# The decode stream ahead of the MLP: a third raw buffer, an earlier start, a pace by stage, and one slot sooner for the even groups' T4 of w_ch2

## Chip, cores and metric

The kernel runs on one core of a Trainium2 chip. The metric is the time of one execution on the device in microseconds (us). One launch does everything: attention, a gated MLP with a spatial projection, and an MLP.

## What is computed

Four batches of 448 tokens, so 1792 tokens of 768 features; 12 heads of 64 in each batch. The weights w_in, w_out, w_ch1 and w_ch2 reach the kernel as fp64 bits, which it decodes to float32 itself. Every product of the gated MLP and of the MLP is made of three TensorE products, of a high and a low part of each side.

```python
attn = 1 / (1 + exp(-(q @ k.T / sqrt(64) - log(448))));  x = attn @ v        # 4 x 12 heads
h = relu(x @ moe_w_in);  u, v = h[..., :512], h[..., 512:]                  # 768 -> 1024
v_n = (v - mean(v)) / sqrt(var(v) + 1e-6)
v_s = einsum('ts,bsd->btd', w_spatial, v_n) + b_spatial[None, :, None]       # over the 448 tokens
x = (u * v_s) @ w_out                                                        # 512 -> 768
xn = (x - mean(x)) / sqrt(var(x) + 1e-6) * g_ln
out = x + relu(xn @ w_ch1) @ w_ch2                                           # 768 -> 3072 -> 768
```

## The kernel before

The stages follow each other on TensorE (PE): attention to about 222 us, then `hv` and `hu` (x times the two halves of w_in, batch by batch), then `spatial` for four batches, then `Project` (the product with w_out, LayerNorm, transposes), then the MLP.

**Spatial.** Each batch has four tiles of 128 features. A tile is 11 matmuls into one of four PSUM banks: three times `mm3` (L359 to L361, high by high, high by low, low by high) and two more, L706 and L707, for the last 64 tokens. L707 reads `t2`, which the last ACT instruction of `vn_make` (L687) writes. DVE multiplies the bank by u (L709) and so frees it for the tile four later.

**Projection.** PE makes 14 blocks of 128 tokens. For each, ACT copies the bank out (`evac`, L745), DVE subtracts the mean and multiplies by g_ln (L755), ACT scales (L758), and PE transposes (L765) the block of two steps before. g_ln is fetched by SP at L1180.

**MLP.** w_ch1 and w_ch2 are cut in 12 groups of 256 hidden features; each group's two products are done by Strassen's seven products of blocks, whose weight operands bear the names 11, 21, 22, T1, T2, T3, T4. A group has 14 slots. A table gives for each operand the slot at which it is made: `=T4` subtracts two blocks on POOL (L829), `T4` splits it in a high part (cast on ACT, L834) and a low part (subtraction on POOL, or with a `v` on DVE, L837). `W1_JOBS` is for w_ch1 (even groups, odd groups), `W2_JOBS` for w_ch2; the slots of `W2_JOBS` count from 14 behind those of `W1_JOBS`, so an even group's w_ch2 operands are made in the same slots as the next, odd group's w_ch1 operands. DVE also sums finished products (L1417) and adds the hidden features (`summed`, L1321; `s_first` L1352 and L1356; `s_add`, L1340; lows at L1308 and L1312), on which PE's next products wait.

**The decode stream.** A weight chunk (128 x 768 as fp64 bits, 768 KB) is loaded by SP at L371, brought to float32 by ACT in two instructions (L405, L410) and by DVE in one (L414). For the first and the even groups' w_ch2, 12 chunks in all, this is done ahead of the MLP by the generator `after_stream`: it decodes a chunk, stores it to a scratch tensor `wfscr` (384 KB, L1086), and the MLP reads it back with `load_plain` (L822). It has two raw buffers in `q_all`, and a chunk's load is issued on SP as the one before the last is done. It advances by one step per `AFTER_US` of PE's modelled time, from `hv` of the last batch on and only while the queue of w_out's decode jobs is empty; SP issues its DMAs in program order, as ACT and DVE do their instructions.

Of the kernel before, what the change touches and what calls it, by code (L numbers as in the profile page):

```python
# [88 lines left out]
PLACE_W_R = [30464, 28672]  # L89
PLACE_F = dict(y=0, gb=6144, tmp=6912, xn=9216, dec=10752)  # L90
# [34 lines left out]
        (-7, "11"), (-6, "=T1"), (-6, "21"), (-5, "T1"), (-5, "=T3"), (-4, "22"), (-3, "=T2"), (-2, "T2"), (0, "T3"),  # L125
        (0, "=T4"), (2, "T4"),
# [4 lines left out]
        (-5, "11v"), (-4, "=T1"), (-4, "22v"), (-4, "=T3"), (-3, "21v"), (-3, "=T2"), (-2, "=T4"), (-1, "T4v"), (1, "T3"),  # L131
# [13 lines left out]
BY_GPSIMD = (0, 2, 4)  # L145
AFTER_US = 1.15
# [150 lines left out]
def sigmoid_attention_gmlp_mlp(ctx: ExitStack, tc, q, k, v, w_in, w_sp, w_out, g_ln, w1, w2, out):  # L297
# [762 lines left out]
    jobs.add([t.split for t in wo_chunks[:2]])  # L1060
    jobs.add([t.decode for t in wo_chunks[2:]] + [t.split for t in wo_chunks[2:]])
    out2_r.free()
    vraw, uraw, vns, g = {}, {}, {}, []
    put_after[0] = 1
    defer[0] = True

    def after_stream():
        parts = [(g, f) for g in PLAIN_W2 for f in range(2)]

        def load(k):  # L1070
            if k < len(parts):
                g, f = parts[k]
                weights[g].load(1, f, raw_r.next())

        load(0)
        load(1)
        for _ in range(4):
            yield
        for k, (g, f) in enumerate(parts):
# [4 lines left out]
            blk = dec_r.next()  # L1084
            weights[g].bits(1, f, blk)
            nc.sync.dma_start(wfscr[g, f], blk.ap(WC))  # L1086
            load(k + 2)
            yield

    after, owed = after_stream(), [0.0]  # L1090

    def go_on(us):
        owed[0] += us
        while owed[0] >= AFTER_US:
            owed[0] -= AFTER_US
            next(after, None)

# [23 lines left out]
    def filled(gen, every, side=(), pace=1.0):  # L1121
        side = iter(side)
        for i, us in enumerate(gen):
            if not jobs.q:
                go_on(pace * (us or 0.0))
# [20 lines left out]
    filled(hv(B - 1), 3, v_norm(0))  # L1146
# [4 lines left out]
    wsp_raw.free()  # L1151
    vraw_r.blocks.append(F.alloc(4 * DH))
# [3 lines left out]
    filled(hu(B - 1), HU_EVERY, vn_first())  # L1156
# [3 lines left out]
    vu["u"].free()  # L1160
    gf_r = Ring(F, S, 2)
    for b in range(B):
        g_alloc((b + 1) * S)
        side = [*([v_norm(2)] if b == 0 else ()), *([vn_at(b + 2)] if b + 2 < B else ())]
        filled(spatial(b, vns[b], wsp, uraw[b], gf_r, g), 2 if b else 1, chain(*side), (0.75, 0.75, 1.1, 1.1)[b])
# [6 lines left out]
    u_in.free()  # L1172
    jobs.drain()
# [39 lines left out]
    for j, (u, c) in enumerate(order):  # L1213
# [10 lines left out]
        if j > 11:  # L1224
            proj.turn_parked(order[j - 2][1], banks, nc.vector.tensor_copy if j < 13 else nc.scalar.copy)
        proj.evac(c, ps, y_at[c])
# [309 lines left out]
    def at(i, slot):  # L1536
        return 14 * i + slot
# [229 lines left out]
```

## Times and profile before

| what | value |
|---|---|
| runs | 1020.75, 1021.31, 3429.54 us; median 1021.31 |
| the profiled execution | 1022.51 us |
| its span | 1020.7 us |
| PE busy | 990.6 us, 97% |
| DVE, ACT, POOL busy | 748.9 (73%), 497.1 (49%), 371.1 (36%) us |
| mean granted clock of PE | 0.994 |
| read from HBM | 168.54 MB |

The span is the stretch from the first to the last instruction of the profiled execution; its own time is 1.8 us more. PE is busy nearly always, so a gain must come from the stretches in which it stands still or runs at the lower clock: the windows of the stages and the list of PE's waits say where these are, and the timelines of the other engines say what it waits for.

### The profile page before, as it was taken

The page shows a single profiled execution, that of the slowest core. Times are in us where ns is not written, and L with a number is a line of the kernel's source. Part 1 is how long each engine was busy: PE and PEld are TensorE (multiplying, and loading weights), DVE is VectorE, ACT ScalarE, POOL GpSimd, SP SyncE. Part 2 cuts the span into 40 slices and gives each one's busy share as a digit, 9 for nine tenths or more (in the row PEclk, how much of TensorE's full clock was granted, in tenths as well). Part 3 has the DMA queues.
Part 4 walks back from the last instruction along what each step waited for, and adds up shares of the span by engine and source line. Part 5 has one row for each costly group of instructions (what it writes and reads, how often), then busy time and mean ns, then how long its engine had stood idle before and what let it go on. Part 6 is the DMA issues. An engine that isn't in the chain of part 4 may idle for free.

```text
span 1020.7 us, 14832 instructions
## 1 busy us (share of the span) xinstructions
PE 990.6 (97%) x5140; PEld 826.0 (81%) x5140; DVE 748.9 (73%) x985; ACT 497.1 (49%) x826; POOL 371.1 (36%) x331
## 2 busy tenths in 40 slices
PE   8999999999888999999999999999999999999997
PEld 5456667678777998887878788778889999999996
DVE  4669898727585787678888889898876676666666
ACT  5756554435565675456656565644422222222221
POOL 3533233101210585456768767675720021000000
PEclk9999999999998999999999999999999999999999
DMA  8875889746866259966859778695979988888884
GB/s 220 241 237 182 301 298 284 272 152 215 300 230 229 93 191 351 373 241 217 317 205 338 272 262 303 209 340 176 342 289 313 318 272 251 248 248 249 252 249 148
DMA packets 98555, 261.04 MB, mean 256 GB/s; under 512 B 13104, under 2 KB 27440, under 8 KB 98352
## 3 DMA queue, kind: packets, MB, share of 16 engines
q1 hardware_dynamic: 93072, 246.67, 71.4%
q0 software_dynamic: 1760, 7.36, 2.2%
q10 hardware_dynamic: 3648, 6.06, 1.7%
q8 instruction: 41, 0.67, 0.3%
q14 instruction: 34, 0.28, 0.1%
HBM read 168.54 MB, written 91.50 MB: 255 GB/s over the span
## 4 chain that ended last, share of the span: by engine, by line
PE 77%; DVE 6%; issue 4%; DMA 4%; POOL 4%; ACT 4%; SPq 0%; ACTq 0%; POOLq 0%; DVEq 0%
PE ps L359 13%; PE ps L361 13%; PE ps L360 13%; PE acc L359 8%; PE acc L360 8%; PE acc L361 8%; PE psa L569 6%; PE ps L529 5%; POOL f_all L829 2%; POOL t_all L837 2%; PE ps L542 1%; DVE f_all L1417 1%; DMA q_all<-in_w 1%; PE psa L556 1%; DVE f_all L414 1%
## 5 line engine op out<-in xcount | busy, mean ns | idle before, releaser
L1417 DVE TENSOR_TENSOR f_all<-acc,f_all 128x1536 f32<-128x1536 f32 (+1 forms) x106 | 164.6, 1553 | 63.0 <-PE acc L361 62.5
L359 PE MATMUL ps<-r_all,t_all 128*128 128x384 f32 (+1 forms) x432 | 156.9, 363 | 4.1 <-DVE f_all L1321 4.1
L361 PE MATMUL ps<-r_all,t_all 128*128 128x384 f32 (+1 forms) x432 | 156.5, 362 | 0.0
L360 PE MATMUL ps<-r_all,t_all 128*128 128x384 f32 (+1 forms) x432 | 156.3, 362 | 0.0
L1299 ACT CAST r_all<-f_all 128x512 fp32r<-128x512 f32 (+1 forms) x144 | 81.5, 568 | 125.9 <-DVE f_all L1340 83.9
L1312 DVE TENSOR_TENSOR r_all<-f_all,r_all 128x512 fp32r<-128x512 f32 (+1 forms) x143 | 110.4, 780 | 38.1 <-ACT r_all L1299 35.4
L837 POOL TENSOR_TENSOR t_all<-f_all,t_all 128x384 fp32r<-128x384 f32 x78 | 90.3, 1161 | 74.4 <-ACT t_all L834 74.2
L359 PE MATMUL ps<-r_all 128*128 128x512 f32 (+2 forms) x249 | 96.8, 389 | 2.7 <-DVE f_all L709 1.8
L361 PE MATMUL ps<-r_all 128*128 128x512 f32 (+2 forms) x249 | 95.0, 382 | 0.0
L829 POOL TENSOR_TENSOR f_all<-f_all 128x384 f32<-128x384 f32 x76 | 88.9, 1173 | 16.8 <-ACT t_all L834 8.8
L360 PE MATMUL ps<-r_all 128*128 128x512 f32 (+2 forms) x249 | 94.9, 381 | 0.0
L359 PEld LDWEIGHTS ps<-r_all,t_all 128*128 128x128 f32 x432 | 81.2, 188 | 13.8 <-DVE f_all L1321 5.7
L360 PEld LDWEIGHTS ps<-r_all,t_all 128*128 128x128 f32 x432 | 81.3, 188 | 8.1
L361 PEld LDWEIGHTS ps<-r_all,t_all 128*128 128x128 f32 x432 | 81.2, 188 | 8.1
L516 ACT ACTIVATE f_all<-ps,bias_s 128x896 f32<-128x896 f32 x70 | 68.3, 1009 | 35.5 <-PE ps L529 15.0
L360 PE MATMUL acc<-r_all,t_all 128*128 128x512 f32 x198 | 78.4, 396 | 0.1
L361 PE MATMUL acc<-r_all,t_all 128*128 128x512 f32 x198 | 78.3, 395 | 0.0
L359 PE MATMUL acc<-r_all,t_all 128*128 128x512 f32 x198 | 78.2, 395 | 0.0
L834 ACT CAST t_all<-f_all 128x384 fp32r<-128x384 f32 x102 | 50.4, 513 | 34.9 <-POOL f_all L829 29.9
L512 POOL TENSOR_TENSOR r_all<-f_all,r_all 128x384 fp32r<-128x384 f32 x22 | 23.6, 1072 | 115.1 <-DVE r_all L508 111.9
L529 PEld LDWEIGHTS ps<-r_all 64*128 64x128 f32 x432 | 37.5, 184 | 29.9 <-issue 16.9
L359 PEld LDWEIGHTS ps<-r_all 128*128 128x128 f32 x249 | 47.2, 189 | 15.4 <-issue 3.8
(209 smaller groups left out, 2218.4 us busy)
## 6 DMA issues: line engine op xcount, KB each, us to landing
t_all<-wscr SPq DMA_DIRECT2D x164, 384.0 KB, 3.8
wscr<-t_all SPq DMA_DIRECT2D x102, 384.0 KB, 4.1
q_all<-in_w SPq DMA_DIRECT2D x42, 768.0 KB, 6.5
wscr<-r_all SPq DMA_DIRECT2D x66, 384.0 KB, 4.6
r_all<-wscr SPq DMA_DIRECT2D x46, 384.0 KB, 3.9
m_all<-in_v SPq DMA_DIRECT2D x24, 256.0 KB, 3.6
yscr<-f_all SPq DMA_DIRECT2D x14, 384.0 KB, 2.6
f_all<-in_k SPq DMA_DIRECT2D x45, 112.0 KB, 3.6
```

The source lines that it names most:

```text
L359: nc.tensor.matmul(ps, lh, rh, start=first, stop=False, skip_group_check=skip)
L360: nc.tensor.matmul(ps, lh, rl, start=False, stop=False, skip_group_check=skip)
L361: nc.tensor.matmul(ps, ll, rh, start=False, stop=last, skip_group_check=skip)
L516: nc.scalar.activation(af, ps[:, :, :S], AF.Sigmoid, bias=bias_s, scale=1.0 / math.sqrt(D))
L529: nc.tensor.matmul(ps[:, j, :S], a[w][rows, kc], a[x][rows], start=(i == 0), stop=(i == 2))
L569: nc.tensor.matmul(a["ps"][rows, :S], a["v"][:, 4 * j + c], af[:, j], start=(p % 2 == 0 and c == 0), stop=(p % 2 == 1 and c == 2),)
L829: eng.tensor_sub(self.f(m, WHERE[m][name]), self.f(m, a), self.f(m, b))
L834: high(t[:, 0], x)
L837: low.tensor_sub(t[:, 1], x, t[:, 0])
L1299: nc.scalar.copy(t[:, 0], self.rt(name))
L1312: (eng or nc.vector).tensor_sub(t[:, 1], self.rt(name), t[:, 0])
L1417: nc.vector.tensor_add(t, x, t)
```

## The change

It has two parts.

The stream: the first chunk's load goes to a third raw buffer (`extra_raw`, in `f_all`) and is issued as attention ends; the next two loads follow the decode of w_out's last two chunks, whose raw buffers they take. A table `THEN` says which load follows which chunk; chunks 7 and 10 use a further place, `late_raw`, once hu's buffers are free. The stream's pace is a factor by stage, `PACE`; a new chunk is begun only while no other job is queued, but a chunk once begun goes on. `go_until(1)` and `go_until(11)` make sure of a count of chunks at two places; `v_load(1)` stands behind the first.

The MLP: in `W2_JOBS` for even groups all jobs of slots -5 to -1 are one slot sooner; in `W1_JOBS` for odd groups six jobs are one or two slots later, and `load_plain` is one slot sooner. No instruction is added or removed on any engine.

```diff
+THEN = {1: 3, 2: 4, 3: 5, 4: 6, 5: 8, 6: 9, 7: 10, 8: 11}
 W1_JOBS = [ ... ,   # the second list is for odd groups
-        (-7, "11"), (-6, "=T1"), (-6, "21"), (-5, "T1"), (-5, "=T3"), (-4, "22"), (-3, "=T2"), (-2, "T2"), (0, "T3"),
-        (0, "=T4"), (2, "T4"),
+        (-7, "11"), (-6, "=T1"), (-6, "21"), (-4, "T1"), (-3, "=T3"), (-3, "22"), (-2, "=T2"), (-1, "T2"), (0, "T3"),
+        (1, "=T4"), (2, "T4"),
 W2_JOBS = [         # the first list is for even groups
-        (-5, "11v"), (-4, "=T1"), (-4, "22v"), (-4, "=T3"), (-3, "21v"), (-3, "=T2"), (-2, "=T4"), (-1, "T4v"), (1, "T3"),
+        (-6, "11v"), (-5, "=T1"), (-5, "22v"), (-5, "=T3"), (-4, "21v"), (-4, "=T2"), (-3, "=T4"), (-2, "T4v"), (1, "T3"),
+PACE = (1.0, 0.8, 0.5, 0.4, 0.4, 1.0)
...
-    jobs.add([t.split for t in wo_chunks[:2]])
-    jobs.add([t.decode for t in wo_chunks[2:]] + [t.split for t in wo_chunks[2:]])
     out2_r.free()
+    extra_raw = F.at(5760, 2 * WC)
+    extra_dec = F.at(9984, WC)
...
+    after_parts = [(g, f) for g in PLAIN_W2 for f in range(2)]
+    def after_load(k):
+        g, f = after_parts[k]
+        weights[g].load(1, f, extra_raw if not k else late_raw if k in (7, 10) else raw_r.next())
     def after_stream():
...
+        def decode_last(k):
+            wo_chunks[2 + k].decode()
+            after_load(1 + k)
+        after_load(0)
+        jobs.add([t.split for t in wo_chunks[:2]])
+        jobs.add([lambda k=k: decode_last(k) for k in range(2)] + [t.split for t in wo_chunks[2:]])
-        for _ in range(4):
+        for _ in range(3):
             yield
-        for k, (g, f) in enumerate(parts):
+        for k, (g, f) in enumerate(after_parts):
+            while k and jobs.q:
+                yield
             weights[g].scale(1, f)
...
-            blk = dec_r.next()
+            blk = dec_r.next() if k else extra_dec
             weights[g].bits(1, f, blk)
             nc.sync.dma_start(wfscr[g, f], blk.ap(WC))
-            load(k + 2)
+            if k in THEN:
+                after_load(THEN[k])
+            count[0] += 1
             yield
+    def go_until(n):
+        while count[0] < n:
+            next(after)
...   # filled()
-            if not jobs.q:
-                go_on(pace * (us or 0.0))
+            go_on(pace * (us or 0.0))
...
-    filled(hv(B - 1), 3, v_norm(0))
+    next(after)
+    filled(hv(B - 1), 3, v_norm(0), PACE[0])
...
+    go_until(1)
+    extra_raw.free()
     v_load(1)
     u_load(1)
-    filled(hu(B - 1), HU_EVERY, vn_first())
+    filled(hu(B - 1), HU_EVERY, vn_first(), PACE[1])
...
+    late_raw = F.at(0, 2 * WC)
+    extra_dec.free()
+    after_load(7)
     for b in range(B):
-        filled(spatial(b, vns[b], wsp, uraw[b], gf_r, g), 2 if b else 1, chain(*side), (0.75, 0.75, 1.1, 1.1)[b])
+        filled(spatial(b, vns[b], wsp, uraw[b], gf_r, g), 2 if b else 1, chain(*side), PACE[2 + b])
...   # projection, step j
+        if j == 2:
+            go_until(11)
...   # MLP
-                plan(at(g, 6 + f), lambda f=f, g=g: weights[g].load_plain(f, dec[2 + f]))
+                plan(at(g, 5 + f), lambda f=f, g=g: weights[g].load_plain(f, dec[2 + f]))
```

Line numbers of the changed kernel are higher: by 2 to L839, by 9 at the stream's store (L1095), by 22 at g_ln's load (L1202), by 24 in the MLP behind it.

On SP, behind the loads of w_out's last chunks (`in_w_out`), the loads of the stream (`in_w`) and the stores of v's rows (`vscr`) and of its statistics (`sscr`) stand so before:

```order
L371 DMA q_all<-in_w_out 128x1536 x2
L636 DMA vscr<-f_all 128x512 x2
L371 DMA q_all<-in_w 128x1536 x2
L636 DMA vscr<-f_all 128x512 x2
L643 DMA sscr<-vraws 128x7x2
```

and so now:

```order
L373 DMA q_all<-in_w_out 128x1536 x2
L373 DMA f_all<-in_w 128x1536
L373 DMA q_all<-in_w 128x1536
L638 DMA vscr<-f_all 128x512
L373 DMA q_all<-in_w 128x1536
L1095 DMA wfscr<-f_all 128x768
L638 DMA vscr<-f_all 128x512 x2
L1095 DMA wfscr<-f_all 128x768
L373 DMA q_all<-in_w 128x1536
L638 DMA vscr<-f_all 128x512
L645 DMA sscr<-vraws 128x7x2
```

Four of the stream's loads and two of its stores now stand ahead of the statistics, where two loads stood.

On ACT, in `hu` of the last batch, the piece with the copy to `t2` (L687, now L689), a chunk's two decode instructions (L405 and L410, now L407 and L412) and the relu of one of hu's tiles (L663, now L665) reads so before:

```order
L681 CAST r_all<-f_all 64x512
L405 ACTIVATE q_all<-q_all 128x768
L410 ACTIVATE q_all<-q_all,bias_d 128x768
L687 COPY r_all<-r_all 64x512
L681 CAST r_all<-f_all 128x512
L663 ACTIVATE f_all<-psa 128x448
L681 CAST r_all<-f_all 128x512 x2
```

and so now:

```order
L683 CAST r_all<-f_all 64x512
L689 COPY r_all<-r_all 64x512
L683 CAST r_all<-f_all 128x512
L407 ACTIVATE q_all<-q_all 128x768
L412 ACTIVATE q_all<-q_all,bias_d 128x768
L665 ACTIVATE f_all<-psa 128x448
L683 CAST r_all<-f_all 128x512 x2
```

The copy to `t2` has gone ahead of the chunk's decode; the relu stands directly behind it.

On DVE, in the MLP at the turn from an odd group to an even one, the piece between two `summed` (L1321, now L1345), with weight lows (L837, now L839; the last of the piece is T4's of w_ch2), reads so before:

```order
L1321 TENSOR_TENSOR f_all<-f_all,ps_3323 128x512
L1308 SCALAR_TENSOR_TENSOR r_all<-ps_3324,r_all 128x512
L1312 TENSOR_TENSOR r_all<-f_all,r_all 128x512
L837 TENSOR_TENSOR t_all<-f_all,t_all 128x384 x2
L1352 SCALAR_TENSOR_TENSOR f_all<-ps_3323,f_all 128x512
L1356 SCALAR_TENSOR_TENSOR f_all<-ps_3323,f_all 128x512
L837 TENSOR_TENSOR t_all<-f_all,t_all 128x384
L1312 TENSOR_TENSOR r_all<-f_all,r_all 128x512 x2
L837 TENSOR_TENSOR t_all<-f_all,t_all 128x384
L1417 TENSOR_TENSOR f_all<-acc,f_all 128x1536
L1340 TENSOR_TENSOR f_all<-f_all 128x512
L1321 TENSOR_TENSOR f_all<-f_all,ps_3323 128x512
```

and so now:

```order
L839 TENSOR_TENSOR r_all<-f_all,r_all 128x384
L1345 TENSOR_TENSOR f_all<-f_all,ps_3323 128x512
L1332 SCALAR_TENSOR_TENSOR r_all<-ps_3324,r_all 128x512
L1336 TENSOR_TENSOR r_all<-f_all,r_all 128x512
L839 TENSOR_TENSOR t_all<-f_all,t_all 128x384
L839 TENSOR_TENSOR r_all<-f_all,r_all 128x384
L1376 SCALAR_TENSOR_TENSOR f_all<-ps_3323,f_all 128x512
L1380 SCALAR_TENSOR_TENSOR f_all<-ps_3323,f_all 128x512
L1336 TENSOR_TENSOR r_all<-f_all,r_all 128x512
L839 TENSOR_TENSOR t_all<-f_all,t_all 128x384
L1336 TENSOR_TENSOR r_all<-f_all,r_all 128x512
L1441 TENSOR_TENSOR f_all<-acc,f_all 128x1536
```

A low of the first chunk (11v) has moved ahead of the first `summed`, and T4's low stands one L1336 sooner, ahead of the long sum L1441 as before.

## Rows read from the trace of the kernel before

**Rows 1.** The page: span, and each engine's busy time.

```profile
span 1020.7 us, 14832 instructions
...
PE 990.6 (97%) x5140; PEld 826.0 (81%) x5140; DVE 748.9 (73%) x985; ACT 497.1 (49%) x826; POOL 371.1 (36%) x331
```

**Rows 2.** Windows by stage: length; PE, PEld, DVE, ACT, POOL; clock, DMA share, GB/s.

```profile
258.90:306.40 47.50, 39.39 (x178) 33.68 (x177) 32.05 (x57) 29.62 (x50) 7.51 (x11) 0.96 0.76 265
306.40:345.00 38.60, 33.69 (x188) 33.25 (x187) 21.38 (x46) 22.05 (x37) 6.63 (x8) 0.91 0.53 191
345.00:765.00 420.00, 413.50 (x1896) 343.08 (x1895) 347.97 (x377) 235.63 (x419) 268.27 (x238) 1.00 0.75 270
765.00:1007.00 242.00, 241.99 (x1377) 241.70 (x1376) 156.91 (x210) 68.92 (x143) 13.67 (x8) 1.00 0.83 260
```

**Rows 3.** PE's waits, 225 to 345 us: total us, times, longest.

```profile
PE psa L765 <- ACT f_all L758: 4.9, 1, 4.9
PE psa L707 <- ACT r_all L687: 3.4, 1, 3.4
PE psa L359 <- DVE f_all L709: 2.9, 3, 1.3
PE ps L359 <- DVE f_all L709: 1.8, 2, 1.5
```

**Rows 4.** Timeline of ACT, 256 to 266 us: start, length, line, [idle before, releaser].

```profile
262.31 0.88 ACT L405 ACTIVATE q_all<-q_all 128x768 f32<-128x768 f32 x1 [4.86 <-DMA q_all<-in_w]
...
263.95 0.60 ACT L687 CAST r_all<-r_all 64x512 fp32r<-64x512 f32 x1
...
264.98 0.54 ACT L663 ACTIVATE f_all<-psa 128x448 f32<-128x448 f32 x1
```

**Rows 5.** Timeline of SP (DMA issues), 238 to 260 us.

```profile
255.33 0.91 SPq L371 DMA_DIRECT2D q_all<-in_w  x1
```

**Rows 6.** Line L371, 225 to 325 us: issue to landing of its 12 loads.

```profile
DMA to landing us min/median/max: 4.4/6.3/10.6
```

**Rows 7.** Windows of PE alone: length, busy (count), clock, DMA share, GB/s.

```profile
264.69:267.77 3.08, 3.08 (x9) 0.51 0.92 338
...
324.26:329.30 5.04, 5.04 (x18) 0.52 0.48 185
329.30:334.00 4.70, 4.70 (x30) 1.00 0.30 116
```

**Rows 8.** Window of all engines ahead of 262.5 us; columns as rows 2.

```profile
255.00:262.50 7.50, 6.28 (x31) 5.47 (x30) 4.70 (x7) 1.52 (x4) 1.83 (x3) 1.00 0.98 298
```

**Rows 9.** Timelines of ACT, SP and DVE in the projection.

```profile
306.82 0.91 ACT L405 ACTIVATE q_all<-q_all 128x768 f32<-128x768 f32 x1 [4.82 <-DMA q_all<-in_w]
...
310.50 0.32 SPq L1086 DMA_DIRECT2D wfscr<-f_all  x1
...
314.74 1.99 SPq L1180 DMA_DIRECT2D f_all<-in_g_ln  x1
...
322.09 1.02 DVE L755 SCALAR_TENSOR_TENSOR f_all<-f_all,mv 128x768 f32<-128x768 f32 x1 [3.89 <-DMA f_all<-in_g_ln]
```

**Rows 10.** PE's waits, 345 to 750 us.

```profile
PE ps L359 <- DVE f_all L1321: 5.1, 4, 1.4
```

**Rows 11.** Timelines of POOL and DVE, 511 to 525 us.

```profile
516.06 3.86 POOL L829 TENSOR_TENSOR f_all<-f_all 128x384 f32<-128x384 f32 x3
...
520.51 0.81 DVE L837 TENSOR_TENSOR t_all<-f_all,t_all 128x384 fp32r<-128x384 f32 x1 [2.43 <-ACT t_all L834]
521.24 1.75 DVE L1417 TENSOR_TENSOR f_all<-acc,f_all 128x1536 f32<-128x1536 f32 x1
...
523.91 0.68 DVE L1321 TENSOR_TENSOR f_all<-f_all,ps 128x512 f32<-128x512 f32 x1
```

**Rows 12.** Timelines of SP and ACT, 503 to 509 us.

```profile
503.11 0.32 SPq L822 DMA_DIRECT2D f_all<-wfscr  x1
...
507.77 1.34 ACT L834 CAST t_all<-f_all 128x384 fp32r<-128x384 f32 x3
```

More of the change, by code (lines that the diff above doesn't have):

```diff
@@ L1065, in sigmoid_attention_gmlp_mlp @@
     defer[0] = True
+    after_parts = [(g, f) for g in PLAIN_W2 for f in range(2)]
+    def after_load(k):
+        g, f = after_parts[k]
+        weights[g].load(1, f, extra_raw if not k else late_raw if k in (7, 10) else raw_r.next())
     def after_stream():
[L1068 to L1076, printed above, removed]
-        for _ in range(4):
+        def decode_last(k):
[5 more added lines that the diff above has]
+        for _ in range(3):
             yield
-        for k, (g, f) in enumerate(parts):
+        for k, (g, f) in enumerate(after_parts):
+            while k and jobs.q:
+                yield
             weights[g].scale(1, f)
@@ L1083, in after_stream @@
             yield
-            blk = dec_r.next()
+            blk = dec_r.next() if k else extra_dec
             weights[g].bits(1, f, blk)
             nc.sync.dma_start(wfscr[g, f], blk.ap(WC))
-            load(k + 2)
+            if k in THEN:
+                after_load(THEN[k])
+            count[0] += 1
             yield
-    after, owed = after_stream(), [0.0]
+    after, owed, count = after_stream(), [0.0], [0]
     def go_on(us):
@@ L1160, in sigmoid_attention_gmlp_mlp @@
     vu["u"].free()
+    late_raw = F.at(0, 2 * WC)
+    extra_dec.free()
     gf_r = Ring(F, S, 2)
+    assert count[0] < 7
+    after_load(7)
     for b in range(B):
@@ L1172, in sigmoid_attention_gmlp_mlp @@
     u_in.free()
+    late_raw.free()
     jobs.drain()
```

## Prediction

> **What bounds the kernel now.** I read the page's busy times first: PE works 990.6 of 1020.7 us [rows 1], so only the 30 us in which it stands still, and the little that it loses at a lower clock, can be won. Next the windows by stage [rows 2]. From 765 us on PE is busy for 241.99 of 242.00 us: nothing is to be had there. The MLP up to 765 leaves 420.00 - 413.50 = 6.5 us, the spatial stage 47.50 - 39.39 = 8.1 us, the projection 38.60 - 33.69 = 4.9 us. The last two run at a mean granted clock of 0.96 and 0.91, where the MLP has 1.00.
>
> Then PE's waits between 225 and 345 us [rows 3]. One wait of 3.4 us in the spatial stage is for ACT's copy to t2 (L687), one of 4.9 us in the projection for ACT's L758, and four of 4.7 us together for DVE's product L709, which frees a bank. The timelines say why. ACT idled 4.86 us ahead of a chunk's decode because its load had not landed; the two instructions of the decode took from 262.31 to 263.95, and only then came the copy to t2 [rows 4]. That load was issued at 255.33 [rows 5], so it took 7.0 us, where L371's loads around it took between 4.4 and 10.6 [rows 6]. In the projection L758 waits for L755 and that for g_ln's load, issued at 314.74 and there at 322.09, 7.35 us later [rows 9].
>
> Both stalls are followed by a stretch at 1.2 GHz, the lower of the clock's two levels: after PE had stood still for 3.4 us, 9 matmuls took 3.08 us at a granted clock of 0.51, and after 4.9 us 18 took 5.04 us at 0.52; the next 30 took 4.70 us at 1.00 [rows 7]. At the fast pace 18 matmuls are 18/30 x 4.70 = 2.82 us, so the clock cost 2.2 us there; in the spatial stage, by the same share (0.44 of the stretch), 1.3 us. The whole stalls are therefore worth 3.4 + 1.3 = 4.7 and 4.9 + 2.2 = 7.1 us.
>
> In the MLP PE has four waits of 5.1 us together, the longest 1.4, all for DVE's summed, L1321 [rows 10]. DVE stood still for 2.43 us ahead of T4's low (L837 at 520.51), since T4's make was the last of three that POOL did back to back (516.06 + 3.86 = 519.92) and ACT's cast follows it; behind the low stand the sum L1417 (1.75 us) and L1340, then L1321 at 523.91 [rows 11]. Had the low not waited, L1321 would have come up to 2.43 us sooner, more than the 1.4 that PE lost.
>
> **The change part by part.** No instruction is added or removed, so what remains is where each waits.
>
> *t2 ahead of the decode.* ACT was idle from 262.31 - 4.86 = 257.45 us. In the new order the copy to t2 comes ahead of the decode that waits, and the chunk decoded ahead of the copy has its load ahead of the statistics in SP's new order, so it is there by then. The copy then ends at about 257.5 + 0.6 = 258.1 [rows 4], and PE wants it only at 264.69 - 3.4 = 261.3 [rows 3, 7]. So the stall goes: 4.7 us won. The wait does not vanish, though. The next decode still needs a load that SP issues behind the statistics' chain, as at 255.33 before [rows 5], and gets it at about 262.3; behind it now stands the relu L665. It ends at 262.3 + 1.64 (the decode, 262.31 to 263.95) + 0.54 = 264.5 us. That relu frees a bank that PE wants one spatial tile after 261.3, that is 11 matmuls of 39.39/178 = 0.22 us later, at 263.7; with the hand-over to PE the new wait is some 1 to 1.8 us, and I take 1.4. It is no longer than the MLP's waits of 1.4, behind which the clock stayed at 1.00 [rows 2, 10], so I add nothing for the clock. The four waits for L709 (4.7 us) I leave, since DVE's and ACT's work per tile is the same and only its order moves. Net 4.7 - 1.4 = 3.3 us. The bounds: nothing, if the later loads merely lend each other time; and all that PE does not work in the stage, 8.1 + 1.3 = 9.4.
>
> *g_ln sooner.* Ahead of its load on SP stood ten of the stream's stores, now nine; the ninth went at 310.50, and its chunk's decode had stood 4.82 us for its load [rows 9]. With chunk 7's load sooner (it goes to the further buffer) that wait should go: the store at about 310.5 - 4.8 = 305.7, the chunk's next load behind it, g_ln at about 306.1 and there 7.35 us later, at 313.5. From there to PE took 324.26 - 322.09 = 2.2 us [rows 7, 9], so PE can go on at 315.7; it wants that at 324.26 - 4.9 - 3.3 = 316.1. The whole 7.1 us are won. If the ninth store stays at 310.5, g_ln is there at 318.3 and PE goes on at 320.5: 4.4 of the 4.9 us remain, and the slow stretch with them, so that the bound below is 0.5 us.
>
> *T4 one slot sooner.* Between 345 and 765 us lie seven groups, so a slot is 420/(7 x 14) = 4.3 us [rows 2]. T4's make and cast move by one slot, and the odd group's makes of T3 and T2, which shared POOL with them, move out of the way. Even if POOL only brings T4's make forward by one of its three, 3.86/3 = 1.3 us of the 1.4 are covered [rows 10, 11]; the chain's start is sooner too. I take all of the waits, 5.1 us; the bounds are 0 and 6.5. 11v's low now stands ahead of a summed, an instruction of 0.8 us (as the low at 520.51) [rows 11] whose operand must be there in time: see the last rival.
>
> *At nothing.* The loads and stores only move; SP has idle time around them. v_load(1) now waits for the first chunk, behind hv's last tiles; its data is used a batch later. If that cover were gone, hu's side work would slip by the length of a load, 4.4 us at least [rows 6].
>
> **The sum.** 3.3 + 7.1 + 5.1 = 15.5 us. The profiled execution's own 1022.51 us become 1007.0; it lies 1.2 above the median of the runs shown, 1021.31, so the runs should lie at 1021.3 - 15.5 = 1005.8 us, or -1.5%. Two per cent, about what a measurement of this kernel can tell from no change, is 20.4 us, so 1000.9 and 1041.7 are the bounds.
>
> **The rivals.**
>
> *A, the sum as it stands:* 1005.8; chance 0.45.
>
> *B, the third buffer only moves the wait.* In the 7.5 us ahead of 262.5 the DMA engines were 0.98 busy [rows 8], while the loads of that stretch took 7.0 us where the shortest took 4.4 [rows 5, 6]. An extra load in flight then takes its time from v's rows and their statistics, which stand on SP behind four loads now, and the copy to t2 itself comes late. The Trainium skill, "DMA: Bandwidth & Descriptors", section "Issuing engines are not separate DMA queues", says that all transfers run on the same 16 DMA engines and interleave; by that rule the buffer buys order and no bandwidth, and the spatial term would be nothing. The trace agrees, with 0.98 and 7.0 against 4.4 us. Against the rival: the first loads now start near 222 us, ahead of that stretch. It gives 1021.3 - 7.1 - 5.1 = 1009.1; chance 0.20.
>
> *C, g_ln is still late,* since spatial's lower pace puts off the ninth chunk: 1021.3 - 3.3 - 5.1 = 1012.9; with 0.5 won, 1012.4; chance 0.15.
>
> *F, the MLP's wait stays:* DVE's new lows take the place of T4's: 1021.3 - 3.3 - 7.1 = 1010.9; chance 0.06.
>
> *D, everything clears.* The lower pace in spatial also frees DVE and ACT of decodes, so that L709 is never late: 1021.3 - 9.4 - 7.1 - 6.5 = 998.3; chance 0.10. The waits for L709, 4.7 us of four, are what has to go [rows 3].
>
> *E, slower.* The read back of a decoded chunk (load_plain, L822) went out at 503.11 and the cast of it is the last of three from 507.77 on, after some 5.5 us [rows 12]. Now the cast and DVE's 11v and 22v come a slot sooner, and so does the load in the table; but it can't be issued before the buffer that it fills is read, which the odd group's late jobs decide, and those moved back. If it lands late by x, DVE waits for it with the summed behind, and PE loses up to x in each of five even groups. From x = 15.5/5 = 3.1 us the change gains nothing; from (15.5 + 20.4)/5 = 7.2 us it is slower by more than 2%, above 1041.7. A slot is 4.3 us, so the first would need most of a slot and the second nearly two. Chance 0.04, half of it over 2%.
>
> **How the numbers follow.** The likeliest is A, 1005.8 us; its own range is 1002 to 1009, by the new bank wait and the L709 waits. For eight in ten A, B, C and F are needed, which reach to 1012.9: 1000 to 1013. Out are D (0.10) and E (0.04). Faster by over 2% is D alone, 0.10; slower by over 2% the half of E, 0.02; the rest, 0.88, is within 2%. The range reaches 1000 rather than 1002 since a part of D may come with A.
>
> **What would show it.** In the profile after: no wait of PE for the copy to t2 (L689), and a new one of 1 to 1.8 us near 263 for an ACT relu (L665) or a bank; the granted clock of spatial and projection at 0.99 or more; g_ln's load (L1202) issued before 308 us; no wait for L760 over 1 us; no waits for L1345 in the MLP, and DVE's idle time ahead of T4's low gone. The forecast is wrong if one of these three stalls stays, above all if PE waits for another ACT or DVE instruction of the stream for 3 us and more with a slow stretch behind, or if DVE waits for ACT's cast of a block read back from wfscr.

## The result

The changed kernel takes 1005.79 us (median of four runs, 1004.95 to 1007.71) against 1021.03 for the kernel before. The ratio goes by the means, 1006.06 against 1020.03 with the one run of 3429.54 us left out: 0.9863, 95% interval 0.9835 to 0.9891, or 11 to 17 us less. The forecast was 1005.8. The profiled execution took 1007.71 us, its span is 1005.9.

The page of the changed kernel, span and busy times; beside [rows 1] PE is busy 5 us less, DVE 7 us less:

```profile
span 1005.9 us, 14819 instructions
...
PE 985.2 (98%) x5140; PEld 824.9 (82%) x5140; DVE 742.0 (74%) x985; ACT 497.8 (49%) x826; POOL 374.0 (37%) x331
```

Windows of the changed kernel, about the stages (columns as [rows 2]: length; PE, PEld, DVE, ACT, POOL busy; clock, DMA share, GB/s):

```profile
259.00:306.00 47.00, 39.39 (x184) 35.17 (x184) 31.77 (x61) 29.29 (x54) 6.04 (x9) 0.93 0.69 246
306.00:345.00 39.00, 39.00 (x237) 38.75 (x236) 26.48 (x54) 24.68 (x39) 14.95 (x16) 1.00 0.47 172
345.00:750.00 405.00, 401.87 (x1825) 331.93 (x1824) 333.68 (x360) 228.46 (x404) 263.29 (x231) 1.00 0.77 277
```

In the projection PE no longer stands still, and the clock is 1.00 where it was 0.91. The spatial stage has hardly changed: 7.6 us without work, where it was 8.1, and its clock is even lower, 0.93 against 0.96. PE's waits from 215 to 345 us and from 345 to 750 us (total us, times, longest; beside [rows 3, 10]):

```profile
PE psa L361 <- ACT f_all L665: 5.9, 1, 5.9
PE psa L361 <- DVE f_all L711: 1.4, 2, 0.9
PE ps L361 <- DVE f_all L711: 0.3, 1, 0.3
...
PE ps L361 <- DMA t_all<-wscr: 1.5, 1, 1.5
```

Three of the four old waits are gone: for the copy to t2 (3.4), for L758 (4.9), for the MLP's summed (5.1). L709's 4.7 us have become 1.7. Two are new: 5.9 us for a relu of hu's tiles, L665, and 1.5 us for the MLP's first weights.

To compare the stages of different executions I take four points on PE's timeline: the start of the last matmul of attention, of spatial's last matmul but one (L706 of the kernel before), of the projection's last transpose (L765), and of PE's last matmul. Lengths between them in us:

| profiled execution | attention ends | to spatial's end | to the last transpose | to PE's end |
|---|---|---|---|---|
| before | 223.9 | 82.2 | 86.2 | 622.1 |
| changed | 222.1 | 80.8 | 79.8 | 617.5 |
| e1 stream alone | 222.5 | 81.1 | 79.6 | 624.7 |
| e2 MLP alone | 223.0 | 81.9 | 84.4 | 615.6 |
| e10 table of w_ch2 alone | 222.4 | 83.4 | 84.4 | 617.1 |
| e11 table of w_ch1 alone | 223.3 | 83.3 | 84.3 | 624.9 |
| e6 decode of chunk 4 late | 221.5 | 79.0 | 82.5 | 618.4 |
| e7 statistics behind the load | 223.0 | 78.9 | 79.8 | 617.6 |
| e8 no stream in hu | 221.9 | 77.5 | 85.8 | 615.7 |
| e12 relu freed of both waits | 221.8 | 73.6 | 82.9 | 617.3 |
| e15 e12 and a free L760 | 223.4 | 74.1 | 80.4 | 615.7 |
| e9 before, g_ln on POOL | 222.3 | 82.2 | 85.8 | 624.8 |
| e14 before, late chunks | 222.7 | 82.9 | 83.9 | 622.5 |
| e13 both of these | 222.9 | 82.6 | 78.9 | 622.8 |

Between the two profiled executions the span's 14.8 us are 1.9 in attention, 1.4 in hv, hu and spatial, 6.5 in the projection, 4.7 in the MLP and 0.4 behind PE's last matmul. But one execution differs from the next by as much as some of these: attention, whose code is the same in all, ends anywhere from 221.5 to 223.9, with the old stream and with the new. So I take means over the rows whose stage is alike. hv to spatial: 82.6 with the old stream (before, e2, e9, e10, e11, e13, e14), 81.0 with the new (changed, e1): 1.7 us less. Projection: 84.8 (before, e2, e10, e11) and 79.7 (changed, e1, e7): 5.1 less. MLP: 623.4 with the old tables (before, e1, e9, e13, e14), 616.8 with both new ones (changed, e2, e6, e7, e8, e12, e15): 6.6 less. That is 13.4 us, and the runs' ratio says 14.0. The mean of the new stream up to spatial rests on two executions alone, so its 1.7 us are the weakest of the three.

### The profile page after: what moved, and what is told of

The parts are those of the page before. It is cut to its first block, busy times and chain, and to the rows that moved or that the text cites. A ratio compares the mean times of both kernels' runs of the same rounds, so it can differ in the third digit from the quotient of the medians.

```text
span 1005.9 us, 14819 instructions
## 1 busy us (share of the span) xinstructions
PE 985.2 (98%) x5140; PEld 824.9 (82%) x5140; DVE 742.0 (74%) x985; ACT 497.8 (49%) x826; POOL 374.0 (37%) x331
## 4 chain that ended last, share of the span: by engine, by line
PE 89%; DMA 3%; DVE 3%; ACT 3%; issue 1%; POOL 1%; SPq 0%; ACTq 0%; DVEq 0%
PE ps L361 15%; PE ps L363 14%; PE ps L362 14%; PE acc L361 10%; PE acc L362 10%; PE acc L363 10%; PE psa L571 6%; PE ps L531 5%; PE ps L544 1%; DMA t_all<-wscr 1%; DMA sscr<-vraws 1%; PE psa L558 1%; DMA q_all<-in_w 1%; DMA f_all<-in_q 0%; PE psa L361 0%
## 5 line engine op out<-in xcount | busy, mean ns | idle before, releaser
L1441 DVE TENSOR_TENSOR f_all<-acc,f_all 128x1536 f32<-128x1536 f32 (+1 forms) x106 | 164.6, 1553 | 66.3 <-PE acc L363 65.8
L361 PE MATMUL ps<-r_all,t_all 128*128 128x384 f32 (+1 forms) x390 | 143.2, 367 | 1.6 <-DMA t_all<-wscr 1.5
L363 PE MATMUL ps<-r_all,t_all 128*128 128x384 f32 (+1 forms) x390 | 142.8, 366 | 0.0
L362 PE MATMUL ps<-r_all,t_all 128*128 128x384 f32 (+1 forms) x390 | 142.5, 365 | 0.0
L1336 DVE TENSOR_TENSOR r_all<-f_all,r_all 128x512 fp32r<-128x512 f32 (+1 forms) x143 | 106.9, 754 | 38.2 <-ACT r_all L1323 35.1
L839 POOL TENSOR_TENSOR t_all<-f_all,t_all 128x384 fp32r<-128x384 f32 x87 | 101.3, 1170 | 79.5 <-ACT t_all L836 70.6
L361 PE MATMUL ps<-r_all 128*128 128x512 f32 (+2 forms) x291 | 109.6, 377 | 0.5 <-DVE f_all L711 0.3
L363 PE MATMUL ps<-r_all 128*128 128x512 f32 (+2 forms) x291 | 108.3, 372 | 0.0
L362 PE MATMUL ps<-r_all 128*128 128x512 f32 (+2 forms) x291 | 108.3, 372 | 0.0
L361 PEld LDWEIGHTS ps<-r_all,t_all 128*128 128x128 f32 x390 | 73.4, 188 | 11.8 <-issue 2.0
L362 PE MATMUL acc<-r_all,t_all 128*128 128x512 f32 x204 | 80.7, 396 | 0.0
L361 PE MATMUL acc<-r_all,t_all 128*128 128x512 f32 x204 | 80.6, 395 | 0.0
L363 PE MATMUL acc<-r_all,t_all 128*128 128x512 f32 x204 | 80.5, 395 | 0.0
L363 PEld LDWEIGHTS ps<-r_all,t_all 128*128 128x128 f32 x390 | 73.4, 188 | 8.4
L362 PEld LDWEIGHTS ps<-r_all,t_all 128*128 128x128 f32 x390 | 73.4, 188 | 8.3
L836 ACT CAST t_all<-f_all 128x384 fp32r<-128x384 f32 x107 | 52.7, 513 | 45.1 <-POOL f_all L831 35.9
L361 PE MATMUL acc<-t_all,r_all 128*128 128x384 f32 x201 | 68.3, 340 | 1.1 <-issue 0.7
L363 PE MATMUL acc<-t_all,r_all 128*128 128x384 f32 x201 | 68.0, 338 | 0.0
L362 PE MATMUL acc<-t_all,r_all 128*128 128x384 f32 x201 | 67.8, 337 | 0.0
## 6 DMA issues: line engine op xcount, KB each, us to landing
m_all<-in_v SPq DMA_DIRECT2D x24, 256.0 KB, 3.3
```

Source lines behind the costliest of these rows:

```text
L361: nc.tensor.matmul(ps, lh, rh, start=first, stop=False, skip_group_check=skip)
L362: nc.tensor.matmul(ps, lh, rl, start=False, stop=False, skip_group_check=skip)
L363: nc.tensor.matmul(ps, ll, rh, start=False, stop=last, skip_group_check=skip)
L836: high(t[:, 0], x)
L839: low.tensor_sub(t[:, 1], x, t[:, 0])
L1336: (eng or nc.vector).tensor_sub(t[:, 1], self.rt(name), t[:, 0])
```

## Experiments

The theory: three stalls are apart from each other; the stream's part won the projection, the MLP's tables the MLP, and in spatial one wait took the place of another. The rivals are told with each.

**e1 and e2, one part each.** e1 is the changed kernel with `W1_JOBS`, `W2_JOBS` and `load_plain` as before, e2 the kernel before with these changed:

```diff
# e1
-                plan(at(g, 5 + f), lambda f=f, g=g: weights[g].load_plain(f, dec[2 + f]))
+                plan(at(g, 6 + f), lambda f=f, g=g: weights[g].load_plain(f, dec[2 + f]))
# e2: the other way round
```

> The changed decode stream with the MLP's tables and the read back as before. Theory (the parts add up): the MLP's four waits for the summed instruction come back, about 5 us, the projection's wait for L760 stays away, PE's wait of 5.9 us for the relu L665 near 262 us stays: 1021.0 - 15.2 + 4.9 = 1010.7 us, ratio to the kernel before 0.990. Rival (the stream's early loads and stores disturb the MLP or the attention, and the tables make up for it): 1014 us or more, ratio 0.993 or more.

> The kernel before with the changed tables and the read back one slot sooner, the stream as before. Theory: the MLP's waits for the summed instruction go (5.1 us), and a wait of 1.5 us for a weight read at the MLP's start stays as in the changed kernel or not; the two stalls of 3.4 and 4.9 us with their slow stretches stay: 1021.0 - 4.7 = 1016.3 us, ratio 0.995. Rival (the tables need the stream's new order, a read back lands late): no gain, 1020 to 1022 us. Attention's end on PE: if the 1.9 us by which it came sooner in the changed kernel's profile are chance, it may fall anywhere from 222.0 to 224.0 us here.

e1 took 1014.04 us, ratio 0.9942 (0.9921 to 0.9964); e2 1012.30, ratio 0.9923 (0.9905 to 0.9942). The product of the two is 0.9866, and the whole change had 0.9863: the parts add up. But they divide otherwise than expected: by the ratios the stream won 6 us instead of 10, and the MLP's tables 8 instead of 5. e1's time lies where its rival had put it, at 1014 us. The rival's reason, that the tables make up for a harm which the early transfers do, does not follow: the parts would then not add up. e1's MLP took 624.7 us, inside the 622.1 to 624.8 of the executions with the old stream and the old tables. PE's wait for summed in e1 (345 us on), and PE's two big waits in e2:

```profile
PE ps L361 <- DVE f_all L1345: 5.1, 4, 1.4
...
PE ps L361 <- DMA t_all<-wscr: 1.0, 1, 1.0
```

```profile
PE psa L765 <- ACT f_all L758: 3.8, 1, 3.8
...
PE psa L707 <- ACT r_all L687: 2.3, 1, 2.3
```

e1 has the summed's 5.1 us again, e2 the two stalls of the stream's stages and no wait for summed. The wait for the MLP's first weights, 1.0 us in e1 and 1.5 in the changed kernel, is in some executions and not in others, with the old stream too (e9 0.4, e11 0.8); I count it to neither part, and what makes it come and go was not tried.

**e10 and e11, one table each,** in the kernel before: e10 has `W2_JOBS` for even groups changed alone, e11 `W1_JOBS` for odd groups alone.

> The kernel before with the changed table of w_ch2's even groups alone (T4 and the others one slot sooner), the odd groups' w_ch1 jobs and the read back as before. Theory (T4's make comes sooner, so its low no longer holds up the sum): the MLP's four waits of 5.1 us go, 1014 to 1016 us against 1019.7, ratio 0.995. Rival (POOL is full with the odd group's makes in the same slots, T4 comes no sooner): the waits stay at 3 us or more in all, ratio 0.997 to 1.002.

> The kernel before with the changed table of w_ch1's odd groups alone (T1, =T3, 22, =T2, T2, =T4 one or two slots later). Theory (this table only makes room): T4's make on POOL comes sooner by the one or two makes that move behind it, 1.3 to 2.6 us, which already covers part of PE's waits of 1.4 us each: waits 0 to 3 us in all, 1015 to 1019 us. Rival (it does nothing by itself or makes w_ch1's operands late): waits for L1321 5 us or more, or a new wait of PE for a weight in odd groups, 1020 us and more.

e10: 1015.39 us, ratio 0.9953 (0.9935 to 0.9970). e11: 1022.55 us, ratio 1.0025 (1.0011 to 1.0038), slower. PE's waits for summed, e10 and then e11:

```profile
PE ps L359 <- DVE f_all L1321: 1.0, 3, 0.4
```

```profile
PE ps L359 <- DVE f_all L1321: 5.8, 4, 1.5
```

The table of w_ch2 is what takes the waits away, all but 1.0 us. It moves T4's two jobs and six others, so that T4's own slot does it is argued, not shown apart. What speaks for it is the place of T4's low on DVE: it starts 12.0 us behind the first summed in the kernel before (508.50, 520.51), 10.1 in e10 (505.46, 515.60) and 8.3 in the changed kernel (499.55, 507.88). DVE still stands idle ahead of it, for 2.43 us in e10 as before and for 1.45 in the changed kernel:

```profile
515.60 0.81 DVE L837 TENSOR_TENSOR t_all<-f_all,t_all 128x384 fp32r<-128x384 f32 x1 [2.43 <-ACT t_all L834]
```

So the idle time did not go; the whole chain comes sooner. The later w_ch1 jobs do nothing for the waits alone, and cost 0.25% (DVE's idle time grows to 3.4 us); on top of the other table, with the read back moved too, the last 1.0 us goes (e2: none left). My guess that they would make room by themselves fell.

**e7, is the load late by its place on SP or by the full DMA engines?** In the changed kernel the decode of chunk 4 (L407) idles until its load lands, and L665 stands behind it. Timelines of ACT and SP:

```profile
253.54 0.62 ACT L689 CAST r_all<-r_all 64x512 fp32r<-64x512 f32 x1
...
265.57 0.88 ACT L407 ACTIVATE q_all<-q_all 128x768 f32<-128x768 f32 x1 [9.46 <-DMA q_all<-in_w]
...
267.20 0.52 ACT L665 ACTIVATE f_all<-psa 128x448 f32<-128x448 f32 x1
```

```profile
244.39 0.38 SPq L645 DMA_DIRECT2D sscr<-vraws  x1
253.75 0.37 SPq L648 DMA_DIRECT2D vstat<-sscr  x1
...
257.50 0.35 SPq L373 DMA_DIRECT2D q_all<-in_w  x1
```

The copy to t2 (L689) is done at 254.2, long before PE wants it. The load went out at 257.50, behind the four reads of the statistics, which waited 9.4 us for their write (244.39 to 253.75). Before, that was 4.5 us:

```profile
247.49 0.38 SPq L643 DMA_DIRECT2D sscr<-vraws  x1
252.04 0.36 SPq L646 DMA_DIRECT2D vstat<-sscr  x1
```

e7 puts these reads behind the store of chunk 2 and the load of chunk 4:

```diff
-                (nc.gpsimd if b < B - 1 else nc.sync).dma_start(vstat[:, i, :3], main)
-                (nc.gpsimd if b < B - 1 else nc.sync).dma_start(vstat[:D, i, 3], sscr[i * S + 3 * P : (i + 1) * S])
+                if b < B - 1:
...
+                else:
+                    stats_late.append((vstat[:, i, :3], main))
+                    stats_late.append((vstat[:D, i, 3], sscr[i * S + 3 * P : (i + 1) * S]))
...
                 after_load(THEN[k])
+            if k == 2:
+                for dst, src in stats_late:
+                    nc.sync.dma_start(dst, src)
```

> The changed kernel, with the four reads of the statistics (L648, L649, which wait on SP for the write sscr) put behind the store of chunk 2 and the load of chunk 4 instead of ahead of them. Theory A (queue: the load was late because it stood on SP behind reads that waited for sscr, 253.7 us): the load goes out by 251 us instead of 257.5, lands by 259, PE's wait for L665 falls from 5.9 us to under 1 and the slow stretch goes: 1005.8 - 7.5 = 998.3 us, ratio 0.978. Theory B (bandwidth: the 16 DMA engines are full in this stretch whatever the order): the load takes over 10 us, lands at 261 us or later, PE waits 2 us or more: 1002 to 1006 us, ratio 0.981 to 0.985.

1004.16 us, ratio 0.9842 (0.9820 to 0.9864), not told apart from the changed kernel's 0.9863. Timeline of SP, and ACT's instruction that waited:

```profile
250.60 0.42 SPq L373 DMA_DIRECT2D q_all<-in_w  x1
```

```profile
264.20 0.88 ACT L407 ACTIVATE q_all<-q_all 128x768 f32<-128x768 f32 x1 [6.71 <-DMA q_all<-in_w]
```

The load went out 7 us sooner and landed 1.4 us sooner: it took 13.6 us instead of 8.0. PE still waited 4.0 us for the relu. Theory A falls: an earlier place on SP does not bring the load in time. Theory B's figures came, but its reason, full DMA engines, is only half of what the trace shows. In the changed kernel the share is 0.99 from 248 to 256 us, where it was 0.57 before, and 0.92 from 256 us on, where it was 0.99 (the columns behind the length are clock, DMA share and GB/s):

```profile
248.00:256.00 8.00, 1.00 0.99 217
256.00:264.00 8.00, 1.00 0.92 308
```

In e7, though, the share was lower for most of the time in which the load stood still:

```profile
252.00:254.00 2.00, 1.00 0.84 133
254.00:256.00 2.00, 1.00 0.69 183
```

The trace's DMA packets say more. From 251.5 to 256.0 us no packet of SP's queue moved in e7, although a store and the load had been issued at 250.22 and 250.60. Nearly all that moved was u's read back, a DMA of POOL's queue. The load's first packet started at 257.0, 6.4 us after its issue, and nearly all of its packets took 234 ns each, as those of the chunk before it. So in e7 the load was late by standing behind other transfers, and not by moving slowly; why SP's queue stood still so long no run here tells.

**e6, the decode behind the relus.** Four more steps of the stream ahead of chunk 4:

```diff
                 yield
+            for _ in range(4 if k == 4 else 0):
+                yield
             weights[g].scale(1, f)
```

> The changed kernel, with the decode of the stream's chunk 4 four steps later, behind the two relus L665 and the second copy to t2 on ACT. Theory (PE's 5.9 us are lost only because the relu stands behind a decode whose load is late): no wait for L665 over 0.5 us and no slow stretch behind it, 7.5 us won in spatial, some given back where later chunks come later: 998 to 1001 us, ratio 0.978 to 0.981. Rival (ACT and DVE only stand still elsewhere): PE waits for L711 instead, 3 us or more, 1003 to 1006 us.

1008.02 us, ratio 0.9881 (0.9861 to 0.9901). PE still waited 4.6 us for L665, and neither side had foreseen for what (ACT):

```profile
265.31 0.54 ACT L665 ACTIVATE f_all<-psa 128x448 f32<-128x448 f32 x1 [9.75 <-DMA uscr<-f_all]
```

With no decode ahead of it, the relu waits for the buffer that it writes. hu's tiles have two buffers, and the store of an earlier tile (uscr, issued at about 257.6) had not landed before 265.2. In the changed kernel this wait lay under the decode's: the store landed at 266.1 us, the decode ended at 267.2. The later chunks also gave 2.7 us back in the projection.

**e8, no transfer of the stream in hu.**

```diff
-PACE = (1.0, 0.8, 0.5, 0.4, 0.4, 1.0)
+PACE = (1.0, 0.0, 0.7, 0.6, 0.6, 1.0)
```

> The changed kernel with another PACE, (1.0, 0.0, 0.7, 0.6, 0.6, 1.0): no step of the stream in hu of the last batch, so that between 243 and 260 us neither a load nor a store of it goes out, and more steps in spatial. Theory (the DMA engines' backlog makes the relu L665 wait, through the stores of u's tiles whose buffers it fills): share of the DMA engines in 248 to 264 us clearly under the 0.99 and 0.92 of the changed kernel, u's stores land within 4 us instead of 8, PE's wait for L665 falls from 5.9 us to under 1, spatial ends 7 us sooner after attention's end (80.8 to 74 us). What is put off has to be made up in projection, where PE may wait 1 to 3 us for L760: 1000 to 1003 us in all, ratio 0.981 to 0.984. Rival (the wait hangs on ACT's order, not on the transfers): PE still waits 3 us or more for L665, 1005 to 1010 us.

1008.84 us, ratio 0.9893 (0.9877 to 0.9910). Two windows and PE's waits in e8:

```profile
248.00:256.00 8.00, 1.00 0.92 198
256.00:264.00 8.00, 1.00 0.59 189
```

```profile
PE psa L361 <- DVE f_all L711: 4.7, 3, 2.4
PE psa L767 <- ACT f_all L760: 4.6, 1, 4.6
```

The DMA share from 256 us on falls from 0.92 to 0.59, u's stores land in a median of 3.0 us instead of 5.2, and PE's wait for L665 is gone altogether. ACT's relu still stood behind a store of u, but only to 261.1 us, where it was 265.3 in e6, which has no decode ahead of it either:

```profile
261.13 0.54 ACT L665 ACTIVATE f_all<-psa 128x448 f32<-128x448 f32 x1 [7.43 <-DMA uscr<-f_all]
```

So far the theory was right, though not in its total, 1000 to 1003. But the decodes that were put off stand ahead of L711 and L760 later: spatial as a whole wins 3.3 us, and the projection gives back 6.0.

**e12, both reasons of the relu's wait taken away:** e6's four steps, and four buffers for hu's tiles.

```diff
+    vu["u"].blocks = vu["u"].blocks + vu["v"].blocks
     filled(hu(B - 1), HU_EVERY, vn_first(), PACE[1])
...
-    vu["u"].free()
+    free_all(vu["u"].blocks[:2])
```

> The changed kernel, with both things taken away that held the relu L665 near 262 us: the decode of chunk 4 four steps later (as in e6), and hu of the last batch writes its tiles into four buffers instead of two (hv's two, idle by then, join), so that no relu waits for the store of an earlier tile. Theory (two waits of the same cause, the full DMA engines, lay one over the other and end within 1 us of each other): PE's wait for L665 falls to under 0.5 us, no slow stretch behind it, spatial ends 73 to 76 us after attention's end instead of 80.8; as in e6 the projection gives back up to 3 us by a wait for L760, and the MLP's start 1.5: 998 to 1003 us, ratio 0.978 to 0.983. Rival (a third thing waits for the transfers there, or PE loses it all to L711 and L760 later, as in e8): 1005 us or more, ratio 0.985 or more.

1002.02 us, ratio 0.9808 (0.9787 to 0.9829). PE's waits ahead of the MLP:

```profile
PE psa L767 <- ACT f_all L760: 2.0, 1, 2.0
PE psa L361 <- DVE f_all L711: 1.5, 2, 0.9
```

No wait for L665, and spatial ends 73.6 us after attention instead of 80.8. The stores of u still took a median of 9.4 us; only nothing waits for them. So the transfers are as slow as ever, and 7.2 us were lost because ACT, in its order, waited for them ahead of work that PE needed. Four buffers without e6's steps were not tried.

**e9, e13 and e14, why the projection's stall went.** All three are the kernel before; e9 has the first edit, e14 the second, e13 both:

```diff
-    nc.sync.dma_start(gb.ap(DM), g_ln.broadcast_to((P, DM)))
+    nc.gpsimd.dma_start(gb.ap(DM), g_ln.broadcast_to((P, DM)))
...
-        go_on(AFTER_US * (1.5 if j < 3 else 1.0))
+        go_on(AFTER_US * (0.5 if j < 3 else 1.0))
```

> The kernel before, with g_ln's load issued on POOL's queue instead of SP's. Theory (the projection's stall is only g_ln's load, that stood on SP behind the ninth and tenth store of the stream): the load goes out at about 306 us, PE's wait for L758 goes from 4.9 us to under 0.5 with the slow stretch behind it, and from spatial's end to the last transpose of the projection it takes 79.5 to 80 us instead of 86.2, 6.5 us less: 1013 to 1015 us. Rival (the changed kernel's lower pace, with less decode on ACT and DVE ahead of L755, does it): the wait stays at 3 us or more, 1018 to 1021 us.

> The kernel before with g_ln's load on POOL's queue, as in e9, and besides the stream's steps in the first three blocks of the projection a third as many (factor 0.5 instead of 1.5), so that chunk 10's bits stand behind L755 and chunk 11's decode behind L758. Theory (the projection's stall had two causes of nearly the same end: g_ln, and the decodes ahead of L755 and L758 that wait for their chunks' loads): PE's wait for L758 falls from 4.3 us to under 1.5, no slow stretch, from spatial's end to the last transpose 80 to 82 us instead of 85.8. Rival (something else holds L758): the wait stays over 3 us and the 85 us too.

> The kernel before with the stream's steps in the projection's first three blocks a third as many, as in e13, but g_ln's load on SP as before. Theory (two causes): g_ln still lands at about 320 us, PE's wait for L758 stays at 3.5 to 5 us with its slow stretch, 85 to 86.5 us from spatial's end to the last transpose. Rival (the decodes alone are the cause): the wait falls to under 1.5 us, 80 to 82 us.

e9: 1021.69 us, ratio 1.0013 (1.0000 to 1.0027): nothing. e14: 1019.92, ratio 0.9991 (0.9978 to 1.0003): no difference either. e13: 1015.05, ratio 0.9942 (0.9922 to 0.9961). In e9 g_ln was issued at 294.0 us and landed 6.5 us later, before the projection began, and PE waited all the same, as e9's rival had it. Timelines of DVE and of ACT in e9, and PE's wait:

```profile
316.29 0.96 DVE L414 SCALAR_TENSOR_TENSOR f_all<-q_all 128x768 uint32<-128x768 uint32 x1 [1.66 <-ACT q_all L410]
317.17 1.01 DVE L755 SCALAR_TENSOR_TENSOR f_all<-f_all,mv 128x768 f32<-128x768 f32 x1
```

```profile
319.41 0.90 ACT L405 ACTIVATE q_all<-q_all 128x768 f32<-128x768 f32 x1 [2.46 <-DVE mv L598]
...
321.05 0.95 ACT L758 ACTIVATE f_all<-f_all,rs 128x768 f32<-128x768 f32 x1
```

```profile
PE psa L765 <- ACT f_all L758: 4.3, 1, 4.3
```

L755 stands behind the bits of chunk 10, and L758 behind the decode of chunk 11, which began at 319.41. Its load went out at 313.10 and landed at 319.31; DVE's L598, which the row names, ended at 319.35, so the row does not tell these two apart. What it shows is that L758, whose input was ready at 318.2, stood behind that decode. Two waits with nearly the same end, then, g_ln's and the decode's. In e13, with both out of the way, there is no wait for L758 at all and the projection takes 78.9 us. In e14, where only the chunks were late, 3.2 us are left, a little under the 3.5 to 5 that were expected:

```profile
PE psa L765 <- ACT f_all L758: 3.2, 1, 3.2
```

**e15, e12 with L760 freed.** In e12 L760 stood behind the decode of chunk 11, which waited for its load. e15 puts this decode behind it:

```diff
-        go_on(AFTER_US * (1.5 if j < 3 else 1.0))
+        go_on(AFTER_US * (1.5 if j < 2 else 0.0 if j == 2 else 1.0))
```

> As e12, and besides the stream takes no step behind block 2 of the projection (1.5 for blocks 0 and 1, 0 for block 2, 1.0 then), so that chunk 11's decode, which waited for its load ahead of the second L760, stands behind it and the copies L777. Theory (the projection's wait is the decode that stands ahead of L760 while its load is under way): PE's wait for L760 falls from 2.0 us to under 0.3, no slow stretch behind it, from spatial's end to the last transpose 79 to 80 us instead of 82.9, 3 us off e12: 998 to 1000 us, ratio 0.976 to 0.979. Rival (PE then meets the MLP's first weights earlier and waits there, as 1.5 us in the changed kernel): 1.5 to 2 us come back, 1000 to 1002 us.

1000.44 us, ratio 0.9792 (0.9768 to 0.9816), faster than both kernels: 0.9792/0.9863 = 0.993 of the changed one, and the two intervals don't meet. PE's waits up to the end of the MLP's stretch, the three largest:

```profile
PE psa L361 <- DVE f_all L711: 1.5, 3, 0.9
PE ps L361 <- DVE f_all L711: 0.7, 1, 0.7
PE acc L1529 <- DVE q_all L1538: 0.5, 1, 0.5
```

The median lies 0.4 us above the theory's 998 to 1000, but there is no wait for L760, and none for the MLP's first weights, the rival's reason, in this execution. The projection takes 80.4 us, 2.5 less than in e12. Against e12 (0.9808) the intervals overlap.

## Why the prediction was right, and where its steps were not

The total was met, but the terms were off in both directions, and one step had half of its mechanism. For the spatial stage the prediction's own sign of being wrong came true: PE waits for another ACT instruction behind the stream for over 3 us (L665, 5.9), with a slow stretch behind, and the stage's clock is 0.93 instead of 0.99.

*t2 ahead of the decode: 3.3 us forecast, 1.4 between the two profiles, 1.7 by the means.* That the 4.7 us of the old stall go held. The new wait was put at 1.4 us; it was 5.9, with a stretch at 1.2 GHz behind it:

```profile
267.78:271.00 3.22, 3.22 (x9) 0.50 0.44 164
```

That is a window of PE in the changed kernel (length, busy, clock, DMA share, GB/s), at half the clock, as in [rows 7]: half of it, 1.6 us, is lost too. The step that failed is the sentence that the next load goes out as at 255.33 and lands at about 262.3. I had the length of a load from the kernel before, 7.0 us, and moved more transfers ahead of it without making it longer: the statistics' write took 9.4 us instead of 4.5, the load went out at 257.5 and landed at 265.5. In the trace's packets the write began 4.2 us after its issue, where it was 0.9 before, behind a load and stores that the change had put ahead of it on SP. The relu then ended 3.2 us later than forecast, at 267.7 instead of 264.5, and PE wanted the bank 1.9 us sooner, at 261.8 instead of 263.7, since attention ended 1.9 us sooner in this execution; the hand-over to PE took 0.5 us less than I had allowed. The item "at nothing", that the loads and stores only move, fails by the same step.

Rival B said that the buffer only moves the wait. e7 (issued 7 us sooner, landed 1.4 us sooner) agrees with it, and so does e8, where fewer transfers landed sooner. The rule that stood beside B, of the Trainium skill, "DMA: Bandwidth & Descriptors", section "Issuing engines are not separate DMA queues", is that the DMAs of all issuing engines interleave on the same 16 DMA engines. As B drew from it, order bought little in e7; but in e7's trace SP's and POOL's DMAs did not interleave from 251.5 to 256.0 us, where SP's stood still. I gave B 0.20 and priced it at nothing won; the 1.4 to 1.7 us lie half-way between that and A's 3.3.

By these waits alone the term would be negative: 4.7 - 5.9 - 1.6 = -2.8. What made it 1.4 is the second step that failed, "the four waits for L709 I leave": they fell from 4.7 to 1.7 us, 3.0 less. That the lower pace of the decodes in spatial does it is argued, not tried alone; e8, with a higher pace there, has 5.4 us of these waits. I had that only in rival D. What is left, 1.2 us, these rows don't assign.

*g_ln sooner: 7.1 forecast, 6.5 between the two profiles, 5.1 by the means.* L1202 went out at 307.3 and landed at 313.0, near the 306.1 and 313.5 that I gave, and PE did not wait; the clock stayed at 1.00. But the reason was half told. e9 shows that g_ln sooner gives nothing alone, e14 that later chunks give next to nothing, e13 that both give all. The changed kernel seems to have both, the second by chunk 10's load into the further buffer, which was issued at 302.04, more than 10 us ahead of its decode; this was not tried in the changed kernel itself. My reading of the list of waits stopped at the wait's last releaser; what would have been next stood in ACT's and DVE's order, one instruction ahead of L755 and L758.

*T4 one slot sooner: 5.1 forecast, 4.7 between the two profiles, 6.6 by the means.* All four waits went. e10 shows that the table with T4's slot does it: 4.1 of the 5.1 us of waits. Not all of the step held: the idle time ahead of T4's low, which was to go, is still 1.45 us. In the changed kernel's profile 1.5 us went to the first weights at the MLP's start. The means show 1.5 us more than the waits that went; where these come from is open.

*At nothing:* rightly, as to v_load(1): PE was busy for all of the 37.00 us from 222 to 259. Rival E did not come: no wait of PE for a cast of a block read back from wfscr. Its price was worked out with a slot of 4.3 us, which is wrong: the four waits for summed of [rows 10] end at 464.4, 524.6, 584.9 and 645.1 us, so two groups take 60.2 us and a slot 2.15. A read back would have had to be late by one and a half slots for no gain, and by more than three for 2% slower.

*The sum.* 15.5 us were forecast, and the runs say 14.0, 11 to 17. By the means the terms were off by 1.6 in spatial and 2.0 in the projection, both too high, and by 1.5 in the MLP, too low. A small slip stands in the working, too: 0.44 of 3.08 us is 1.4, not 1.3. That the medians agree to 0.01 us is chance: the median of before was 0.3 us lower in the runs that were compared, and the terms' errors partly cancel.

## What to carry to other kernels

A wait has a list of reasons, not one: before a fix is priced, take the named releaser away on paper and ask what stands next ahead of the waiting instruction on its engine and when its own data lands (here g_ln and a chunk's load were there within 2 us of each other, and the store and the decode ahead of a relu were over within 1.1). When transfers are moved into a stretch that is already full, let each of them land later in the sum, and count the engine that waits for one in program order as lost for everything behind it. Putting such a wait behind the work that PE needs (e12, e15) brought the ratio to 0.9792, where another order of the transfers (e7) left it at 0.9842.

## What the runs showed of the hardware that I had not expected

A full share of the DMA engines says little of the bytes: in the changed kernel 0.99 moved 217 GB/s between 248 and 256 us, and in e8 0.92 moved 198, where elsewhere 0.96 to 1.02 went with 329 to 392 GB/s (380 to 420 us of the changed kernel). The packets of the trace say which transfer held the engines from 248 to 256 us: 0.59 of the changed kernel's 0.99 is u's read back on POOL's queue, 128 packets of 7168 bytes at a mean of 589 ns each. The statistics, whose packets are of 8 bytes and take 9 ns each, hold 0.09. The same read back took 335 and 330 ns a packet in the kernel before and in e2, and 549 to 738 ns in e6, e7, e8 and e12. With the new stream it runs while the statistics' write is still under way, with the old one it starts when that has landed; that this is the cause was not tried.

After a wait of PE the granted clock does not follow from the wait's length alone in these rows: it stayed at 1.00 behind a wait of 2.4 us in e8 and of 1.6 us in e6, and fell to the lower level behind 2.0 us in e12 (a mean of 0.65 over the 2 us around the end of the wait) and behind 2.3 us in e2 (0.50).
